# Five-block rounds for all groups, and attention scores from rounded parts after the eighth job

## Chip, cores, metric

The kernel runs on one core of a Trainium2 chip. The metric is the device time of one execution in microseconds (us), the median of several executions. All tensors in memory are float32. On TensorE a product can be taken in full float32, which runs as two passes, or on operands in F32R, a rounded form of float32, in one pass.

## What is computed

An attention whose softmax keeps only scores within `tau` of the row's maximum, and then two dense two-layer networks on its output. Batch 4, 8 heads, 576 positions, head width 64; 2304 tokens, model width 512, inner width 2048.

```python
scores = scale * np.matmul(q, k.transpose(0, 1, 3, 2))
thresh = np.max(scores, axis=-1, keepdims=True) - tau
scores = np.where(scores >= thresh, scores, -1000000000.0)
attn = np.exp(scores - np.max(scores, axis=-1, keepdims=True))
attn = attn / (np.sum(attn, axis=-1, keepdims=True) + 1e-09)
x = np.matmul(attn, v)                    # -> (2304, 512)
h = x @ w_in                              # first network
x = np.where(h >= 1, h, np.where(h <= -1, 0.0, (h + 1) ** 2 / 4)) @ w_out
h = x @ w_in2                             # second network
out = (h * np.clip(h + 3.0, 0.0, 6.0) / 6.0) @ w_out2
```

## The kernel before

**Attention** is cut into 16 jobs, numbered from 0: one batch and one pair of heads each. A job has five blocks of queries: four of 128 and a last one of 64. For a block, `em_scores` takes the products of queries and keys in float32 (line 335). The two heads lie on the two halves of the 128 partitions, so a product uses 64 rows of TensorE's array, and the two heads' products, which write to different PSUM banks, are issued in turn. In the fifth block each product uses a quarter of the array (64 rows, 64 columns). VectorE then takes the row minimum of the negated scores (348), ScalarE the exponential (360), VectorE masks and sums (369), TensorE turns the result (284), ScalarE copies it out (397), and TensorE multiplies by the values (433).

Queries and keys have to be turned before a job. Jobs 0 to 3 (`JT = 4`) do this on TensorE with 5 and 6 transposes, and ScalarE copies the result out of PSUM. From job 4 on they are loaded in strips 32 wide (`strips`, line 227, twelve DMA issues per job), VectorE's 32x32 transposes turn them (lines 293 and 309), and GpSimd scales the queries (295).

**Dense layers.** Every dense product is made of three products of rounded parts: high x high, high x low, low x high. Weights are loaded and split into parts `wih`, `wil`, `woh`, `wol` by `split_a` and `split_b` (ScalarE 118, 121 or 125 and 139; VectorE 129 and 135; GpSimd 122, 137 and 141). Raw weights stand in a ring of `RAW` = 3 buffers, and of `MORE` = 2 others while attention runs. `split_x` splits the inputs (ScalarE 656, VectorE 657).

**Beside attention**, once job 3 is done, the first network's first ten inner blocks of 128 (`NF1 = 10`) are worked off for six groups of 256 tokens. `em_h` makes an inner block (twelve products of 256 columns, line 676, then the activation, 685 to 694, with high and low parts `gh`, `gl`). `em_part` adds it to one half of the model width (six products, line 738) in the one PSUM bank Q3. When a round's last inner block is in, the bank is emptied and stored as `x2p`; a round that continues an earlier one first loads the earlier sum into `before` and adds it (747). `ROUNDS` lists the rounds in order. The list `steps` says which halves follow which inner block, at a distance set by `OFF`; from it follows `HOLD`, the number of buffers of `gh` and of `gl`, which is 12.

**Afterwards** the rest of the first network and the second network run on 512 tokens at a time (lines 676 and 718).

**Order of work.** Each engine runs its instructions in order. `attention()` and `dense1()` are generators that are stepped alternately; a scheduler then orders the instructions of each engine by priority and by when its own model has them ready. Pins (`after`, `pin_mlp`) tie some of them together. All loads and stores here go through SyncE's queue in order.

Of the kernel before, what the change touches and what calls it, by code (L numbers as in the profile page):

```python
# [8 lines left out]
F32 = mybir.dt.float32  # L9
F32R = mybir.dt.float32r  # L10
ACTF = mybir.ActivationFunctionType
ALU = mybir.AluOpType
# [6 lines left out]
def kernel(  # L19
# [13 lines left out]
    V, S, G, T = nc.vector, nc.scalar, nc.gpsimd, nc.tensor  # L33
    NB, NH, SEQ, D = q.shape
# [4 lines left out]
    MAIN = 512  # L39
    TAIL = SEQ - MAIN  # L40
    HS = SEQ // 2
    GRP = 256

    NG = (NB - 1) * MAIN // GRP
# [2 lines left out]
    NW = len(WIDE)  # L47
    NF1 = 10
    NAT = 1
    JT = 4  # L50
    MLAG = 2
    RAW = 3
    MORE = 2

    const = ctx.enter_context(tc.tile_pool(name="const", bufs=1))
    wbase = ctx.enter_context(tc.tile_pool(name="wbase", bufs=1))
# [7 lines left out]
    taus = const.tile([128, 4], F32, name="taus")  # L64
# [9 lines left out]
    def f32(ap):  # L74
        return ap.bitcast(F32)
# [130 lines left out]
    ap = att_es.enter_context(tc.tile_pool(name="att", bufs=1))  # L206
    mode = {"mlp": False, "att": True, "step": False, "t": 0, "s": 0, "n": 0}

    qn = ap.tile([128, 5, 128], F32, name="qn")
    kn = ap.tile([128, 5, 128], F32, name="kn")  # L210
    vn = [ap.tile([128, 5, 2, D], F32, name=f"vn{i}") for i in range(2)]
    qt, kt = {}, {}
    rp = ap.tile([128, 32], F32, name="rp")
    rq = ap.tile([128, 32], F32, name="rq")
    G.memset(rp, 0.0)
# [18 lines left out]
    def load_q(j):  # L234
        if j >= NJ:
            return
        E = nc.sync if j else nc.scalar
        b, hp = jobs[j]
        for h in HEADS:
            src = q[b, 2 * hp + h]  # L240
            if j >= JT:
                strips(qn, 0, src, h)
                continue
            E.dma_start(out=qn[:, 0:4, h * D:(h + 1) * D], in_=rows(src, b))
        if j < JT:
            E.dma_start(out=qn[0:TAIL, 4, :].rearrange("p (h d) -> p h d", h=2), in_=both(q, j))
# [27 lines left out]
    readers = {}  # L274
# [5 lines left out]
    def reads(x, ago=0):  # L280
        readers[(mode["s"] - ago) % 2] = x

    def turn(out, in_, pin):
        x = T.transpose(out, in_, ident)  # L284
        if pin:
            pe_pins.append(x)

    def unit_q(j):
        if j >= NJ or j in qt:
            return  # L290
        qt[j] = ap.tile([128, SEQ], F32, tag="qt", name="qt", bufs=2)
        if j >= JT:
            V.transpose(out=qt[j], in_=qn.rearrange("p c n -> p (c n)")[:, 0:SEQ])
            load_q(j + 1)
            G.tensor_scalar(out=qt[j], in0=qt[j], scalar1=taus[:, 1:2], scalar2=None, op0=ALU.mult)
            return
        tm = unit_bank().rearrange("p e n -> p (e n)")
        for c in range(5):
            turn(tm[:, c * 128:(c + 1) * 128], qn[:, c, :], c == 0)
        load_q(j + 1)  # L300
        reads(S.activation(out=qt[j], in_=tm[:, 0:SEQ], func=ACTF.Copy, scale=taus[:, 1:2]))

    def unit_k(j):

        if j >= NJ or j in kt:
            return
        kt[j] = ap.tile([128, SEQ + TAIL], F32, tag="kt", name="kt", bufs=2)
        if j >= JT:
            V.transpose(out=kt[j], in_=kn.rearrange("p c n -> p (c n)"))
            load_k(j + 1)  # L310
            return
        tm = unit_bank().rearrange("p e n -> p (e n)")
        for i, c in enumerate((4, 0, 1, 2, 3, 4)):
            turn(tm[:, i * 128:(i + 1) * 128], kn[:, c, :], i == 0)
        load_k(j + 1)
        reads(S.activation(out=kt[j], in_=tm[:, 128 - TAIL:128 + MAIN + TAIL], func=ACTF.Copy))
# [4 lines left out]
    def em_scores(j, i):  # L321

        last = i == NBLK - 1

        if not last:
            mode["s"] += 1
        ss = [unit_bank() for _ in range(1 if last else 2)]
        prev = None
        c = slice(i * 128, i * 128 + (TAIL if last else 128))
        for x, (h, e) in enumerate(((0, 0), (1, 1), (0, 1), (1, 0)) if last else ((0, 0), (1, 0), (0, 1), (1, 1))):  # L330
            r = slice(h * D, (h + 1) * D)
            k0 = e * HS + (TAIL if last or h == 0 else 0)
            o = ss[0][h * TAIL:(h + 1) * TAIL, e, 0:HS] if last else ss[h][:, e, 0:HS]
            with tc.high_priority(offset=900 if x else 0):
                mm = T.matmul(o, qt[j][r, c], kt[j][r, k0:k0 + HS], start=True, stop=True, skip_group_check=True)  # L335
            after(mm, prev)
            prev = mm
            if x == 0:
                pe_pins.append(mm)
                for y in range(1 if last else 2):  # L340
                    after(mm, readers.get((mode["s"] - y) % 2), True)
        nm = ap.tile([128, 2], F32, tag="nm", name="nm", bufs=3)
        th = ap.tile([128, 2], F32, tag="th", name="th", bufs=3)
        p = ap.tile([128, 2, 2, HS], F32, tag="p", name="p", bufs=3)
        if i == 0:
            zt[j] = ap.tile([128, 9], F32, tag="z", name="z", bufs=2)
        for x, s in enumerate(ss):
            reads(V.tensor_scalar(out=p[:, x], in0=s[:, :, 0:HS], scalar1=-1.0, scalar2=3e38,  # L348
                                           op0=ALU.mult, op1=ALU.min, accum_out=nm[:, x:x + 1]), len(ss) - 1 - x)
        blk[j, i] = (p, nm, th, [])  # L350

# [437 lines left out]
                nc.sync.dma_start(out=out[b * SEQ + MAIN:(b + 1) * SEQ, :], in_=ob[64 * e:64 * e + 64, :])  # L789

    HALF = NF1 // 2
    ROUNDS = [(g, list(range(f, f + HALF))) for f in (0, HALF) for g in range(2)]
    ROUNDS += [(g, list(range(NF1))) for g in range(2, NG)]
    before = {}
    hs = [(r, f) for r, (g, fs) in enumerate(ROUNDS) for f in fs]
    n_h = len(hs)
    outs = [(r, half, f) for r, (g, fs) in enumerate(ROUNDS) for half in range(2) for f in fs]
    OFF = NF1 + 2 * MLAG - 3
    steps, o = [], 0
    while o < len(outs):  # L800
        n = len(steps)
# [94 lines left out]
    V.tensor_scalar(out=taus[:, 3:4], in0=taus[:, 2:3], scalar1=0.0, scalar2=3e38, op0=ALU.is_lt, op1=ALU.mult)  # L896
    V.tensor_scalar(out=taus[:, 1:2], in0=taus[:, 2:3], scalar1=0.0, scalar2=0.125, op0=ALU.is_ge, op1=ALU.mult)
    V.tensor_tensor(out=taus[:, 0:1], in0=taus[:, 2:3], in1=taus[:, 3:4], op=ALU.max)
    warm = [None]

    def warm_up(n):
# [38 lines left out]
    for _ in attention():  # L940
# [11 lines left out]
        while credit > 0:  # L952
            c = next(part1)
# [98 lines left out]
```

## Time and profile before

| | us |
|---|---|
| median of three runs | 1119.1 (1118.22 to 1119.16) |
| profiled execution, its own time | 1118.67 |
| its span, first to last instruction | 1116.9 |
| mean granted clock of TensorE | 0.992 |

| engine | busy us | share of the span |
|---|---|---|
| TensorE matmul (PE) | 1087.4 | 97% |
| TensorE weight load (PEld) | 882.1 | 79% |
| VectorE (DVE) | 583.3 | 52% |
| ScalarE (ACT) | 614.0 | 55% |
| GpSimd (POOL) | 438.4 | 39% |

Busy time is that in which at least one instruction of the engine is recorded. Matmuls are pipelined, so their records overlap: how long one occupies the engine is the distance from its start to the next start, not its duration. Each record of a float32 product is one pass, so the 320 score products have 640 records. The shares are means over stages with different limits; the stretches of the profile tell more.

### The profile page before, as it was taken

The numbers are of one execution on the slowest core, as the hardware profiler recorded it, in microseconds if no ns is written. First come the engines' busy times: TensorE is split into PE (matmuls) and PEld (weight loads), VectorE is DVE, ScalarE is ACT, GpSimd is POOL, SyncE is SP. The second block draws the span as 40 slices with busy tenths as digits, with TensorE's granted clock in tenths as the row PEclk, the third lists the DMA queues.
The fourth block names the chain that finished last, engine by engine and source line by source line (L and its number), as shares of the span: only waits on it lengthen the run. The fifth ranks groups of instructions, "written<-read, shape, count | busy, mean of one in ns | idle before, by whom it ended". The sixth has DMA issues, their size and how long they took to land.

```text
span 1116.9 us, 17595 instructions
## 1 busy us (share of the span) xinstructions
PE 1087.4 (97%) x6478; PEld 882.1 (79%) x6478; DVE 583.3 (52%) x1204; ACT 614.0 (55%) x1215; POOL 438.4 (39%) x382
## 2 busy tenths in 40 slices
PE   7998889999999999999999999999999999999998
PEld 5555667777878877888889888888888888898886
DVE  5899887876666656355536765558411111211111
ACT  5777886866667666556557766555432222333222
POOL 0233767622222111155627566567522222222221
PEclk9999889999999999999999999999999999999999
DMA  6454445433222110025222544533010110010001
GB/s 165 118 100 107 124 120 150 103 93 74 63 59 62 43 43 22 12 67 170 77 94 78 157 143 145 158 114 111 24 38 1 33 38 1 10 38 8 13 1 38
DMA packets 140230, 84.26 MB, mean 75 GB/s; under 512 B 99440, under 2 KB 123248, under 8 KB 140144
## 3 DMA queue, kind: packets, MB, share of 16 engines
q1 hardware_dynamic: 138800, 82.84, 27.0%
q8 instruction: 51, 0.84, 0.3%
q10 hardware_dynamic: 1344, 0.30, 0.1%
q14 instruction: 35, 0.29, 0.1%
HBM read 65.73 MB, written 17.37 MB: 74 GB/s over the span
## 4 chain that ended last, share of the span: by engine, by line
PE 88%; DVE 7%; ACT 2%; POOL 1%; issue 1%; SPq 1%; DMA 0%; DVEq 0%; POOLq 0%; ACTq 0%
PE Q L676 35%; PE P L718 28%; PE Q L738 7%; PE Q L433 6%; PE P L335 6%; PE Q L284 5%; DVE p L348 2%; DVE p L369 2%; ACT e L360 1%; DVE xl L657 1%; SPq L227 0%; PE Q L904 0%; DVE th L363 0%; DVE w_c L135 0%; DMA w_raw<-in_moe_w_out_dram 0%
## 5 line engine op out<-in xcount | busy, mean ns | idle before, releaser
L694 POOL TENSOR_TENSOR gl<-r,gh 128x512 fp32r<-128x512 f32 (+1 forms) x190 | 202.6, 1067 | 501.0 <-ACT gh L693 500.5
L676 PE MATMUL Q<-xh,wih 128*128 128x512 f32 (+1 forms) x760 | 262.0, 345 | 0.9 <-DVE r L687 0.7
L676 PE MATMUL Q<-xl,wih 128*128 128x512 f32 (+1 forms) x760 | 257.1, 338 | 0.0
L676 PE MATMUL Q<-xh,wil 128*128 128x512 f32 (+1 forms) x760 | 256.8, 338 | 0.0
L690 DVE SCALAR_TENSOR_TENSOR r<-r,Q 128x512 f32<-128x512 f32 (+1 forms) x80 | 50.7, 633 | 249.4 <-ACT r L689 249.3
L693 ACT ACTIVATE gh<-r 128x512 fp32r<-128x512 f32 (+1 forms) x190 | 99.9, 526 | 125.3 <-PE P L718 53.2
L676 PEld LDWEIGHTS Q<-xh,wih 128*128 128x128 f32 x760 | 144.1, 190 | 24.3 <-issue 4.2
L676 PEld LDWEIGHTS Q<-xl,wih 128*128 128x128 f32 x760 | 144.2, 190 | 16.0
L676 PEld LDWEIGHTS Q<-xh,wil 128*128 128x128 f32 x760 | 144.0, 190 | 15.5
L348 DVE TENSOR_SCALAR_CACHE_REDUCE p<-P 128x576 f32<-128x576 f32 x144 | 104.0, 751 | 53.3 <-PE Q L284 41.0
L369 DVE SCALAR_TENSOR_TENSOR p<-p,th,e 128x576 f32<-128x576 f32 x144 | 122.8, 873 | 15.1 <-ACT e L360 9.5
L689 ACT ACTIVATE r<-Q,three 128x512 f32<-128x512 f32 (+1 forms) x80 | 51.4, 643 | 142.9 <-PE Q L676 138.3
L360 ACT ACTIVATE e<-p,nm 128x576 f32<-128x576 f32 x144 | 108.9, 775 | 34.5 <-DVE p L348 33.6
L687 DVE SCALAR_TENSOR_TENSOR r<-r,Q 128x256 f32<-128x256 f32 (+1 forms) x110 | 54.8, 498 | 125.7 <-ACT r L686 122.4
L284 PE MATMUL Q<-ident,p 128*128 128x128 f32 x656 | 107.9, 282 | 9.8 <-ACT Gf L397 6.5
L718 PE MATMUL P<-woh,gh 128*128 128x512 f32 x288 | 111.9, 390 | 0.6 <-DVE ob L776 0.6
L718 PE MATMUL P<-wol,gh 128*128 128x512 f32 x288 | 112.2, 390 | 0.0
L718 PE MATMUL P<-woh,gl 128*128 128x512 f32 x288 | 111.0, 390 | 0.0
L335 PE MATMUL P<-kt,qt 64*128 64x288 f32 (+1 forms) x640 | 99.5, 429 | 11.0 <-DVE p L348 9.0
L284 PEld LDWEIGHTS Q<-ident,p 128*128 128x128 f32 x656 | 73.6, 141 | 46.3 <-ACT Gf L397 14.0
L137 POOL TENSOR_TENSOR w_c<-w_c,w_raw 128x512 int32<-128x512 int32 x64 | 89.5, 1400 | 41.3 <-DVE w_c L135 23.0
L397 ACT ACTIVATE Gf<-Q 128x512 f32<-128x512 f32 x128 | 74.4, 596 | 33.5 <-PE Q L284 32.8
(91 smaller groups left out, 1840.1 us busy)
## 6 DMA issues: line engine op xcount, KB each, us to landing
w_raw<-in_moe_w_in_dram SPq DMA_DIRECT2D x32, 512.0 KB
w_raw<-in_moe_w_out_dram SPq DMA_DIRECT2D x32, 512.0 KB
vn<-in_v_dram SPq DMA_DIRECT2D x32, 128.0 KB
x2p<-ob SPq DMA_DIRECT2D x16, 256.0 KB
x2d<-ob SPq DMA_DIRECT2D x16, 256.0 KB
xst<-x2d SPq DMA_DIRECT2D x16, 256.0 KB
out_dram<-ob SPq DMA_DIRECT2D x16, 256.0 KB
xst<-xd SPq DMA_DIRECT2D x15, 256.0 KB
```

Of the source, the lines that this page charges most:

```text
L137: x = G.tensor_tensor(out=c.bitcast(I32), in0=c.bitcast(I32), in1=r, op=ALU.add)
L284: x = T.transpose(out, in_, ident)
L335: mm = T.matmul(o, qt[j][r, c], kt[j][r, k0:k0 + HS], start=True, stop=True, skip_group_check=True)
L348: reads(V.tensor_scalar(out=p[:, x], in0=s[:, :, 0:HS], scalar1=-1.0, scalar2=3e38, op0=ALU.mult, op1=ALU.min, accum_out=nm[:, x:x + 1]), ...
L360: pins["S"] = S.activation(out=e, in_=p[:, x], func=ACTF.Exp, bias=nm[:, x:x + 1], scale=-1.0)
L369: pins["M"] = V.scalar_tensor_tensor(out=p[:, x], in0=p[:, x], scalar=th[:, x:x + 1], in1=e, op0=ALU.is_le, op1=ALU.mult, accum_out=zt[j][ ...
L397: S.activation(out=f[:, h, :, d0:d0 + 128], in_=tm.rearrange("p (c n) -> p c n", c=4), func=ACTF.Copy)
L676: mm = T.matmul(h, l[:, kk * 128:(kk + 1) * 128], r, start=(x == 0), stop=(x == 3 * KD - 1))
L693: x = S.activation(out=gh, in_=r, func=ACTF.Copy)
L694: y = G.tensor_tensor(out=gl, in0=r, in1=f32(gh), op=ALU.subtract)
L718: T.matmul(a, l, r, start=(first and x == 0), stop=(last and x == 2))
L738: mm = T.matmul(o, l, r, start=(f == fs[0] and x == 0 and i == 0), stop=(f == fs[-1] and x == 2 and i == 1), skip_group_check=True)
```

## The change

`JT` goes from 4 to 8: jobs 4 to 7 turn queries and keys on TensorE too. From job 8 on, `split_t` turns an operand on VectorE into a buffer `raw`, ScalarE copies it rounded (`qt`, `kt`), and GpSimd subtracts to get the low part (`ql`, `kl`). GpSimd's scaling of the queries goes; the factor moves into the negation after the scores (`taus[:, 3:4]`). A block's scores are then three rounded products for each one before: `qt` x `kt`, `qt` x `kl`, `ql` x `kt`. In the fifth block the two heads' queries stand in one operand with zeros beside them, so that a product uses the whole array.

`ROUNDS` now gives each of the six groups two rounds of five inner blocks, two groups in turn. `OFF` is 9, and `HOLD` comes out as 8. `MORE` is 1: one raw weight buffer less while attention runs.

```diff
-    JT = 4
+    JT = 8
...
-    MORE = 2
+    MORE = 1
...
             if j >= JT:
-                strips(qn, 0, src, h)
+                strips(qn, 0, src[0:MAIN, :], h)
+                strips(qn, 16 + 2 * h, src[MAIN:SEQ, :], h)
...
+    def split_t(nat, hi, name):
+        raw = ap.tile([128, SEQ + TAIL], F32, tag="raw", name="raw")
+        lo = ap.tile([128, SEQ + TAIL], F32R, tag=name, name=name, bufs=2)
+        V.transpose(out=raw, in_=nat.rearrange("p c n -> p (c n)"))
+        S.activation(out=hi, in_=raw, func=ACTF.Copy)
+        G.tensor_tensor(out=lo, in0=raw, in1=f32(hi), op=ALU.subtract)
+        return lo
...
-            V.transpose(out=qt[j], in_=qn.rearrange("p c n -> p (c n)")[:, 0:SEQ])
+            ql[j] = split_t(qn, qt[j], "ql")
             load_q(j + 1)
-            G.tensor_scalar(out=qt[j], in0=qt[j], scalar1=taus[:, 1:2], scalar2=None, op0=ALU.mult)
...
-            V.transpose(out=kt[j], in_=kn.rearrange("p c n -> p (c n)"))
+            kl[j] = split_t(kn, kt[j], "kl")
...
+        thirds = j >= JT
+        whole = thirds and last
+        terms = ((qt, kt), (qt, kl), (ql, kt)) if thirds else ((qt, kt),)
+        for pair in (((0, 0),), ((0, 1),)) if whole else (es[0:2], es[2:4]):
+            for n, (a, w) in enumerate(terms):
+                for h, e in pair:
+                    r = slice(0, 128) if whole else slice(h * D, (h + 1) * D)
...
+                        mm = T.matmul(o, a[j][r, cs], w[j][r, k0:k0 + HS], start=(n == 0), stop=(n == len(terms) - 1),
+                                      skip_group_check=True)
...
-    ROUNDS = [(g, list(range(f, f + HALF))) for f in (0, HALF) for g in range(2)]
-    ROUNDS += [(g, list(range(NF1))) for g in range(2, NG)]
+    ROUNDS = [(g, list(range(f, f + HALF))) for b in range(NG // 2) for f in (0, HALF) for g in (2 * b, 2 * b + 1)]
...
-    OFF = NF1 + 2 * MLAG - 3
+    OFF = 9
```

The order in which TensorE gets its instructions shows at three places. First the scores of the first block of job 9; `P_3206` and `P_3207` are the PSUM tiles of the two heads. Before:

```order
L335 MATMUL P_3206<-kt,qt 128x288
L335 MATMUL P_3207<-kt,qt 128x288
L335 MATMUL P_3206<-kt,qt 128x288
L335 MATMUL P_3207<-kt,qt 128x288
L284 MATMUL Q_3067<-ident,p 128x128 x4
```

In the changed kernel the same block, with the heads' tiles `P_3297` and `P_3298`:

```order
L356 MATMUL P_3297<-kt,qt 128x288
L356 MATMUL P_3298<-kt,qt 128x288
L356 MATMUL P_3297<-kl,qt 128x288
L356 MATMUL P_3298<-kl,qt 128x288
L356 MATMUL P_3297<-kt,ql 128x288
L356 MATMUL P_3298<-kt,ql 128x288
L356 MATMUL P_3297<-kt,qt 128x288
L356 MATMUL P_3298<-kt,qt 128x288
L356 MATMUL P_3297<-kl,qt 128x288
L356 MATMUL P_3298<-kl,qt 128x288
L356 MATMUL P_3297<-kt,ql 128x288
L356 MATMUL P_3298<-kt,ql 128x288
```

Two products per head became six, still in turn between the heads. Second, the fifth block of job 8 on TensorE, between products of `em_part`. Before:

```order
L738 MATMUL Q_2931<-gh,wol_2580 128x256
L335 MATMUL P_3073<-kt,qt 64x288 x4
L284 MATMUL Q_2989<-ident,p 128x128 x4
L738 MATMUL Q_2931<-gh,woh_2579 128x256
L738 MATMUL Q_2931<-gl,woh_2579 128x256
```

In the changed kernel, with `P_3176` as the PSUM tile of both heads:

```order
L762 MATMUL Q_2949<-gh,wol_2717 128x256
L356 MATMUL P_3176<-kt,qt 128x288
L356 MATMUL P_3176<-kl,qt 128x288
L356 MATMUL P_3176<-kt,ql 128x288
L356 MATMUL P_3176<-kt,qt 128x288
L356 MATMUL P_3176<-kl,qt 128x288
L356 MATMUL P_3176<-kt,ql 128x288
L285 MATMUL Q_3105<-ident,p 128x128
```

Four products on quarters of the array became six on the whole of it. Third, TensorE ahead of the scores of job 6, where `kn` are the keys as loaded. Before, VectorE turns them, and TensorE has only the work of earlier blocks there:

```order
L738 MATMUL Q_1738<-gl,woh_1488 128x256
L738 MATMUL Q_1738<-gh,wol_1489 128x256
L284 MATMUL Q_1752<-ident,p 128x128 x4
L335 MATMUL P_1921<-kt,qt 128x288
L335 MATMUL P_1922<-kt,qt 128x288
```

In the changed kernel:

```order
L285 MATMUL Q_1746<-ident,p 128x128
L285 MATMUL P_1899<-ident,kn 128x128 x6
L457 MATMUL Q_1750<-Gf,vn_97 64x256 x8
L457 MATMUL Q_1750<-Gt,vn_97 64x256 x2
L285 MATMUL Q_1790<-ident,p 128x128 x4
L356 MATMUL P_1931<-kt,qt 128x288
```

The six transposes of the keys (`P_1899`) are added ahead of the scores; the five of the queries stand some twenty rows earlier.

## Rows read from the trace of the kernel before

**Rows 1.** Busy time by stretch: us, then busy us (instructions) of each engine
```profile
0.00:107.00 107.00, 94.38 (x661) 60.32 (x661) 87.51 (x238) 78.02 (x158) 27.73 (x35) 1.00 0.52 122
107.00:210.00 103.00, 91.26 (x638) 69.41 (x638) 88.22 (x195) 79.91 (x176) 72.97 (x62) 0.92 0.51 132
210.00:470.00 260.00, 258.96 (x2021) 208.06 (x2019) 162.29 (x438) 169.15 (x376) 61.63 (x64) 1.00 0.22 54
...
520.00:1117.00 597.00, 592.80 (x2881) 500.88 (x2879) 215.47 (x295) 257.48 (x450) 251.13 (x203) 1.00 0.21 65
```

**Rows 2.** Waits of TensorE, 107 to 210 us: total, times, longest
```profile
PE Q L284 <- ACT Gf L397: 4.0, 5, 1.6
PE P L335 <- DVE p L348: 3.4, 2, 2.1
...
PE Q L738 <- DVE ob L751: 1.4, 1, 1.4
```

**Rows 3.** Waits of TensorE, 210 to 470 us
```profile
PE Q L676 <- DVE r L687: 0.7, 2, 0.5
```

**Rows 4.** Timeline of TensorE around a fifth block: start us, us
```profile
233.73 0.28 PE L676 MATMUL Q<-xh,wil 128*128 128x256 f32 x1
...
234.09 0.28 PE L676 MATMUL Q<-xh,wil 128*128 128x256 f32 x1
...
234.56 0.37 PE L738 MATMUL Q<-gh,woh 128*128 128x256 f32 x1
...
234.88 0.28 PE L738 MATMUL Q<-gh,wol 128*128 128x256 f32 x1
235.09 1.19 PE L335 MATMUL P<-kt,qt 64*64 64x288 f32 x8
...
236.62 0.36 PE L738 MATMUL Q<-gh,woh 128*128 128x256 f32 x1
```

**Rows 5.** Timeline of TensorE, first and last of nine products of 512 columns
```profile
639.65 0.39 PE L676 MATMUL Q<-xh,wil 128*128 128x512 f32 x1
...
641.46 0.39 PE L676 MATMUL Q<-xl,wih 128*128 128x512 f32 x1
```

**Rows 6.** Timeline of TensorE and its weight loads in another block
```profile
302.98 1.24 PE L335 MATMUL P<-kt,qt 64*128 64x288 f32 x8
...
303.33 0.65 PE L335 MATMUL P<-kt,qt 64*128 64x288 f32 x4
...
303.57 0.65 PE L335 MATMUL P<-kt,qt 64*128 64x288 f32 x4
...
303.33 0.44 PEld L335 LDWEIGHTS P<-kt,qt 64*128 64x128 f32 x4
```

**Rows 7.** Timeline of TensorE before job 3, transposes
```profile
64.32 0.82 PE L284 MATMUL P<-ident,kn 128*128 128x128 f32 x6
64.98 0.71 PE L284 MATMUL Q<-ident,p 128*128 128x128 f32 x5
```

**Rows 8.** Groups by form: count, busy us, mean ns, idle before
```profile
L694 POOL TENSOR_TENSOR gl<-r,gh 128x512 fp32r<-128x512 f32 x98 | 131.0, 1338 | 267.5 <-ACT gh L693 267.2
...
L657 DVE TENSOR_TENSOR xl<-xu,xh 128x256 fp32r<-128x256 f32 x29 | 12.8, 474 | 1.7 <-ACT xh L656 1.7
...
L309 DVE STREAM_TRANSPOSE kt<-kn 128x640 f32<-128x640 f32 x12 | 9.7, 805 | 0.1
...
L316 ACT ACTIVATE kt<-P 128x640 f32<-128x640 f32 x4 | 2.9, 724 | 0.7 <-PE P L284 0.7
```

**Rows 9.** Chain of work that ended last, 60 to 215 us: start us, us
```profile
103.22 0.69 DVE qt L293
103.92 0.72 DVE kt L309
...
133.10 3.86 DMA w_raw<-in_moe_w_out_dram
...
165.05 2.20 POOL qt L295
```

More of the change, by code (lines that the diff above doesn't have):

```diff
@@ L211 @@
     vn = [ap.tile([128, 5, 2, D], F32, name=f"vn{i}") for i in range(2)]
-    qt, kt = {}, {}
+    qt, kt, ql, kl = {}, {}, {}, {}
     rp = ap.tile([128, 32], F32, name="rp")
@@ L290, in unit_q @@
             return
-        qt[j] = ap.tile([128, SEQ], F32, tag="qt", name="qt", bufs=2)
+        qt[j] = ap.tile([128, SEQ + TAIL], F32R if j >= JT else F32, tag="qt", name="qt", bufs=2)
         if j >= JT:
-            V.transpose(out=qt[j], in_=qn.rearrange("p c n -> p (c n)")[:, 0:SEQ])
+            ql[j] = split_t(qn, qt[j], "ql")
             load_q(j + 1)
-            G.tensor_scalar(out=qt[j], in0=qt[j], scalar1=taus[:, 1:2], scalar2=None, op0=ALU.mult)
             return
@@ L300, in unit_q @@
         load_q(j + 1)
-        reads(S.activation(out=qt[j], in_=tm[:, 0:SEQ], func=ACTF.Copy, scale=taus[:, 1:2]))
+        if j == JT - 1:
+            G.memset(qn[0:64, 4, 64:128], 0.0)
+            G.memset(qn[64:128, 4, 0:64], 0.0)
+        reads(S.activation(out=qt[j][:, 0:SEQ], in_=tm[:, 0:SEQ], func=ACTF.Copy, scale=taus[:, 1:2]))
     def unit_k(j):
@@ L306, in unit_k @@
             return
-        kt[j] = ap.tile([128, SEQ + TAIL], F32, tag="kt", name="kt", bufs=2)
+        kt[j] = ap.tile([128, SEQ + TAIL], F32R if j >= JT else F32, tag="kt", name="kt", bufs=2)
         if j >= JT:
-            V.transpose(out=kt[j], in_=kn.rearrange("p c n -> p (c n)"))
+            kl[j] = split_t(kn, kt[j], "kl")
             load_k(j + 1)
@@ L329, in em_scores @@
         c = slice(i * 128, i * 128 + (TAIL if last else 128))
[L330 to L341, printed above, removed]
+        thirds = j >= JT
+        whole = thirds and last
+        es = ((0, 0), (1, 1), (0, 1), (1, 0)) if last else ((0, 0), (1, 0), (0, 1), (1, 1))
+        terms = ((qt, kt), (qt, kl), (ql, kt)) if thirds else ((qt, kt),)
+        x = 0
+        for pair in (((0, 0),), ((0, 1),)) if whole else (es[0:2], es[2:4]):
+            for n, (a, w) in enumerate(terms):
+                for h, e in pair:
+                    r = slice(0, 128) if whole else slice(h * D, (h + 1) * D)
+                    k0 = e * HS + (TAIL if last or h == 0 else 0)
+                    if whole:
+                        o, cs = ss[0][:, e, 0:HS], slice(MAIN, MAIN + 128)
+                    else:
+                        o, cs = ss[0][h * TAIL:(h + 1) * TAIL, e, 0:HS] if last else ss[h][:, e, 0:HS], c
+                    with tc.high_priority(offset=900 if x else 0):
+                        mm = T.matmul(o, a[j][r, cs], w[j][r, k0:k0 + HS], start=(n == 0), stop=(n == len(terms) - 1),
+                                      skip_group_check=True)
+                    after(mm, prev)
+                    prev = mm
+                    if x == 0:
+                        pe_pins.append(mm)
+                        for y in range(1 if last else 2):
+                            after(mm, readers.get((mode["s"] - y) % 2), True)
+                    x += 1
         nm = ap.tile([128, 2], F32, tag="nm", name="nm", bufs=3)
@@ L347, in em_scores @@
         for x, s in enumerate(ss):
-            reads(V.tensor_scalar(out=p[:, x], in0=s[:, :, 0:HS], scalar1=-1.0, scalar2=3e38,
+            reads(V.tensor_scalar(out=p[:, x], in0=s[:, :, 0:HS],
+                                           scalar1=taus[:, 3:4] if j >= JT else -1.0, scalar2=3e38,
                                            op0=ALU.mult, op1=ALU.min, accum_out=nm[:, x:x + 1]), len(ss) - 1 - x)
@@ L898 @@
     V.tensor_tensor(out=taus[:, 0:1], in0=taus[:, 2:3], in1=taus[:, 3:4], op=ALU.max)
+    V.tensor_scalar(out=taus[:, 3:4], in0=taus[:, 1:2], scalar1=-1.0, scalar2=None, op0=ALU.mult)
     warm = [None]
```

## The prediction

> **What bounds the kernel now.** I read the stages first, from the view of busy time by stretch. Attention has the chip to itself until about 107 us, it gets company from the first dense layer until about 470, and from there on everything is dense. In [rows 1] the reader is to see TensorE: 94.4 of 107 us, then 91.3 of 103 with a mean granted clock of 0.92, then 259.0 of 260 and 592.8 of 597. In the second stretch VectorE is busy for 88.2 of 103 us and GpSimd for 73.0, far more than later. I call 107 to 210 us the ramp: weights are split there while the first dense groups already wait for them.
>
> Second, who makes TensorE wait. In the ramp these are single stalls of up to 2 us behind ScalarE and VectorE [rows 2]. From 210 to 470 us there are two entries, the larger of 0.7 us [rows 3]. So from 210 us on each matmul removed or added moves the end by what it occupies, and other engines count only if they become late enough to stop TensorE. Before 210 us an engine's time counts where it lies on the chain of work.
>
> Third, what a matmul occupies. Busy time does not tell this, because records overlap; distances between starts do. A rounded (F32R) matmul of 256 columns takes (234.09 - 233.73)/3 = 0.12 us [rows 4], one of 512 columns (641.46 - 639.65)/8 = 0.226 us [rows 5]. Scores in full float32 run as two passes, in pairs: the two heads on the two halves of the array's rows start together, and the next pair of passes starts 0.24 us later (303.33 to 303.57) [rows 6].
>
> **Scores of jobs 8 to 15.** These 40 blocks lie from 210 to 450 us, where TensorE is full. What a block costs today: from the product at 234.88 to that at 236.62 lie 1.74 us; the same stretch without scores (one rounded product and four transposes, 234.09 to 234.56) takes 0.47; so a block takes 1.27 us [rows 4]. Four pair slots of 0.24 make 0.96 of it. The other 0.31 us is the price of a visit: entering and leaving the mode with the array cut in two.
>
> A changed block has six pair slots of one pass. Nothing in the trace shows a rounded matmul on half of the rows. From the two rounded prices, 288 columns take 0.120 + 32/256 x (0.226 - 0.120) = 0.133 us. The bounds are 0.12 (half of a float32 pass pair) and 0.266 (the two heads one after the other). I take 0.133, because the float32 pairs run side by side without loss: 6 x 0.133 = 0.80 us in place of 0.96. Four cut blocks in each of eight jobs: 32 x 0.16 = **5.1 us less**. The fifth block of a job becomes six whole-array products, also 0.80 us, with no visit: 8 x (1.27 - 0.80) = **3.8 us less**. The order lists hold 104 runs in the cut mode before and 94 after; eight of the ten are those blocks, two more merge: 2 x 0.31 = **0.6 us less**.
>
> One thing could spoil the short slots: each pass needs its own weights. In [rows 6] the loads for the next passes start at 303.33 with the running passes on the same rows and are over by 303.77, before the passes that need them at 303.81 or so: they are hidden. Only the first load after the mode change shows, 0.35 - 0.24 = 0.11 us. With slots of 0.133 a load of 0.11 still fits, but barely.
>
> The Trainium skill (TensorE: Matmul & The Clock Gate, "The mechanism") states that a weight load overlaps running matmuls only when it goes to another row group. The float32 passes here don't bear that out, since their loads overlap on the same rows; no row shows it for rounded halves. By the rule each slot would hold 0.133 + 0.11 us, and the sum would come out slower; I count that as a rival below.
>
> **Transposes of jobs 4 to 7.** JT = 8 moves four jobs' queries and keys from VectorE's transposes to TensorE: 5 + 6 per job, 44 in all. Six take 64.98 - 64.32 = 0.66 us [rows 7], so 44 x 0.11 = **4.8 us more**, part before 107 us and part in the ramp. ScalarE's two copies replace VectorE's two transposes (about 0.72 against 0.80 us each [rows 8]). VectorE is on the chain with them at 103 us: 0.69 + 0.72 = 1.4 us [rows 9]. Those I count as **1.4 us less**. The bounds of this gain are nothing and all eight transposes, 8 x 0.80 = 6.4 us; I stay low, since at the other three jobs I don't find the pair next to each other on the chain.
>
> **Preparing the parts (jobs 8 to 15).** Per operand one transpose of 0.80 us on VectorE, one copy of about 0.72 on ScalarE, and one subtraction on GpSimd, by the subtraction of 128x512 about 1.338 x 640/512 = 1.67 us [rows 8]. GpSimd loses the scaling of the queries (2.2 us in the ramp [rows 9]). One buffer "raw" serves both operands, so they go one after the other: 2 x (0.80 + 0.72 + 1.67) = 6.4 us. The order lists prepare a job's operands while the job before it is scored, some 25 us ahead, so that is covered; uncovered it would be 6.4 us per job. ScalarE gains 16 x 0.72 = 11.5 us, against 91 us free from 210 to 470 [rows 1]. Cost: nothing.
>
> **Rounds.** Groups 2 to 5 now take two rounds each. No matmul is added. Added are 16 splits of inputs (VectorE 0.47 us each [rows 8], 7.6 us, ScalarE about as much), eight more emptied accumulators with their stores, and eight loads of earlier sums. VectorE has 98 us free there, so these are hidden if they come in time. The load has some 7 us (five half steps of six products, 0.72 us each, and 2.5 inner blocks of twelve, 1.44 us each) before its sum is needed; a weight load twice its size takes 3.9 us [rows 9]. The price where it fails: 1.4 us, the one visible wait for an emptied bank [rows 2]. Taken: nothing; bounds nothing and 8 x 1.4 = 11 us.
>
> **One weight buffer less.** Today five weights are loaded ahead. A late load costs up to 3.9 us [rows 9], an early one nothing. Four ahead still cover about 25 us at the ramp's pace (16 weights in 103 us), so I take nothing. The plain loads of jobs 4 to 7 also spare SyncE's queue the strips, which I price at nothing, since TensorE's waits don't name it.
>
> **The sum.** 5.1 + 3.8 + 0.6 + 1.4 - 4.8 = 6.1 us less. The profiled execution took 1118.67 us for a span of 1116.9, and the median of the runs is 1119.1; less 6.1 this gives 1112.6 against the one and 1113.0 against the other. I forecast **1113 us**.
>
> **Rivals.**
> *Short slots don't stay short* (slower). If loads are exposed, 32 x 6 = 192 slots grow by 0.11 us: +21.1, so 1134 us. If the heads run one after the other, by 0.133: +25.5, so 1138.5 us. It turns the change into a loss from a slot of 0.133 + 6.1/192 = 0.165 us on. For it: a slot leaves 0.02 us of slack. Against it: the float32 pairs. Chance 0.13.
> *The ramp grows.* GpSimd gets 2 x 1.67 us for job 8 in place of 2.2, a weight comes late once (3.9), and the clock, whose 0.92 cost (1 - 0.92) x 103 = 8.2 us, drops for a third as long again (2.7): +7.7, so 1121 us. For it: VectorE at 86% and GpSimd at 71% there. Against it: jobs 5 to 7 relieve both. Chance 0.15.
> *The ramp shrinks*: all of VectorE's eight transposes turn into time, 6.4 - 1.4 = 5.0 us more gained, so 1108 us. For it: the waits on VectorE in [rows 2]. Chance 0.12.
> *Banks empty late*: three waits of 1.4 us for sums that aren't loaded, so 1117 us. Chance 0.10.
>
> **How the numbers follow.** The forecast has 0.50, and a range of its own of 1109 to 1116. The shrinking ramp reaches to about 1105, the growing one and the late banks to 1122; beyond lie the long slots (0.13) and tails of 0.06. So the range is 1105 to 1122. Within 0.2% of 1119.1 is 1116.9 to 1121.3, about what a measurement of this kernel can tell from no change. Faster: 0.50 + 0.12 + 0.04 of the growing ramp + 0.04 of the late banks = 0.70. Same: 0.06 + 0.06 = 0.12. Slower: 0.13 + 0.05 = 0.18.
>
> **What will show it.** Cut blocks of jobs 8 to 15 with pair starts 0.13 us apart, and the fifth block 0.80 us from its first product to the next work. Job 8's scores starting within 4 us of 210. TensorE's waits from 210 to 470 still about 1 us, with no new entry for an emptied bank. I am wrong if pair starts lie 0.17 us or more apart, or if job 8 starts after 216 us.

## The result, and the profile after

| | before | after |
|---|---|---|
| median, us | 1119.13 | 1125.26 |
| lowest to highest of four runs | 1118.22 to 1119.73 | 1124.6 to 1126.52 |
| span of the profiled execution | 1116.9 | 1123.8 |

By the medians the changed kernel is slower by 6.1 us; the ratio is 1.0061, its 95% interval 1.0048 to 1.0073. The forecast was 6.1 us faster.

The stretches first, in the columns of [rows 1]:

```profile
0.00:107.00 107.00, 94.72 (x679) 61.42 (x680) 84.47 (x232) 80.21 (x162) 22.87 (x33) 1.00 0.45 114
107.00:210.00 103.00, 84.30 (x602) 63.73 (x601) 83.56 (x178) 76.39 (x161) 62.52 (x56) 0.97 0.48 127
210.00:470.00 260.00, 253.77 (x2148) 217.70 (x2147) 190.32 (x479) 190.83 (x426) 78.90 (x77) 0.99 0.28 72
```

In the ramp TensorE is busy for 84.3 us in place of 91.3. Part of this is its higher mean clock (0.97 against 0.92): in these traces it worked at the lower level for 14.1 us before and 6.8 us after, and half of the difference, some 3.6 us, is time that the same work no longer takes. Every other engine is busy for less time too, so none became the bound there; more of the stretch is spent waiting. From 210 to 470 us TensorE has 6.2 us free, where it had 1.0 before. Who it waits for, from 107 to 210 us and then from 210 to 245:

```profile
PE P L285 <- DVE p L371: 3.5, 2, 2.2
PE Q L285 <- ACT Gf L421: 3.5, 3, 2.1
PE Q L700 <- DVE r L711: 2.9, 3, 1.4
PE P L356 <- DVE p L371: 2.2, 3, 1.0
PE Q L762 <- DVE ob L775: 2.1, 2, 1.5
PE Q L457 <- ACT Gf L424: 2.1, 1, 2.1
...
PE Q L285 <- ACT xu L463: 2.5, 1, 2.5
PE P L356 <- DVE p L371: 1.9, 1, 1.9
```

The first row is new against [rows 2]: the transposes of queries and keys (285) wait for a PSUM bank that VectorE's row minimum (371) has not yet emptied. From 245 to 470 us only 0.7 us of waits are left. From 160 to 240 us, where the table below puts most of the added loss, the largest rows name other work:

```profile
PE Q L285 <- ACT xu L463: 3.7, 2, 2.5
PE Q L700 <- DVE r L711: 2.8, 3, 1.4
PE Q L762 <- DVE ob L775: 2.1, 2, 1.5
...
PE P L285 <- DVE p L371: 1.3, 1, 1.3
```

So TensorE waits there for several kinds of ScalarE's and VectorE's work, and the transposes' bank is 1.3 us of it.

What a matmul occupies came out as forecast. First a block of job 9, then a fifth block, in the timeline of TensorE:

```profile
256.86 0.28 PE L762 MATMUL Q<-gh,wol 128*128 128x256 f32 x1
257.06 0.40 PE L356 MATMUL P<-kt,qt 64*128 64x288 f32 x2
257.30 0.30 PE L356 MATMUL P<-kl,qt 64*128 64x288 f32 x2
257.44 0.30 PE L356 MATMUL P<-kt,ql 64*128 64x288 f32 x2
257.57 0.30 PE L356 MATMUL P<-kt,qt 64*128 64x288 f32 x2
257.71 0.29 PE L356 MATMUL P<-kl,qt 64*128 64x288 f32 x2
257.84 0.29 PE L356 MATMUL P<-kt,ql 64*128 64x288 f32 x2
258.06 0.66 PE L285 MATMUL Q<-ident,p 128*128 128x128 f32 x4
...
279.79 0.29 PE L356 MATMUL P<-kt,qt 128*128 128x288 f32 x1
...
280.58 0.27 PE L285 MATMUL Q<-ident,p 128*128 128x128 f32 x1
```

Pairs start (257.84 - 257.30)/4 = 0.135 us apart, and the fifth block takes 280.58 - 279.79 = 0.79 us. Only the first slot after the mode change is longer, 0.24 us.

To set work against waiting I priced every start of a TensorE instruction by what it occupies at the full clock: 0.12, 0.133 and 0.227 us for rounded products of 256, 288 and 512 columns, 0.24 for a float32 pair, 0.11 for a transpose, 0.155 for each entry to or exit from the array cut in two. What lies between starts beyond that is lost time. Work and lost time are estimates by these prices, good to some 0.5 us.

| us | work | lost | lost 0-110 | 110-160 | 160-240 | after 240 |
|---|---|---|---|---|---|---|
| before | 1065.6 | 45.6 | 21.0 | 13.6 | 7.8 | 3.1 |
| after | 1060.4 | 57.5 | 17.8 | 14.9 | 18.9 | 6.0 |

The change took 5.2 us of work off TensorE, as forecast (its terms of work add up to 5.1 + 3.8 + 0.6 - 4.8 = 4.7), and added 11.9 us in which TensorE has nothing ready or runs at the lower clock. Of this 11.1 us lie from 160 to 240 us, 1.3 from 110 to 160 and 2.9 behind 240, against 3.2 saved before 110 us.

### The profile page after: what moved, and what is told of

Read it like the earlier page. It is cut to its first block, busy times and chain, and to the rows that moved or that the text cites. A ratio compares the mean times of both kernels' runs of the same rounds, so it can differ in the third digit from the quotient of the medians.

```text
span 1123.8 us, 18063 instructions
## 1 busy us (share of the span) xinstructions
PE 1082.1 (96%) x6634; PEld 892.0 (79%) x6634; DVE 604.5 (54%) x1221; ACT 635.1 (57%) x1255; POOL 440.5 (39%) x388
## 4 chain that ended last, share of the span: by engine, by line
PE 78%; DVE 8%; ACT 6%; issue 3%; POOL 3%; DMA 2%; SPq 0%; DVEq 0%; POOLq 0%; ACTq 0%
PE Q L700 30%; PE P L742 25%; PE Q L457 6%; PE P L356 6%; PE Q L762 6%; PE Q L285 5%; DVE p L371 2%; DVE p L393 2%; POOL w_c L137 1%; ACT e L384 1%; DVE w_c L135 1%; ACT Gf L421 1%; POOL gl L718 1%; DMA qn<-in_q_dram 1%; ACT r L709 1%
## 5 line engine op out<-in xcount | busy, mean ns | idle before, releaser
L393 DVE SCALAR_TENSOR_TENSOR p<-p,th,e 128x576 f32<-128x576 f32 x144 | 127.9, 912 | 15.8 <-ACT e L384 9.4
L356 PE MATMUL P<-kt,qt 64*128 64x288 f32 (+2 forms) x464 | 78.1, 407 | 11.0 <-DVE p L371 9.0
L762 PE MATMUL Q<-gh,woh 128*128 128x256 f32 x240 | 75.1, 313 | 2.4 <-DVE ob L775 2.1
```

Source lines behind the costliest of these rows:

```text
L356: mm = T.matmul(o, a[j][r, cs], w[j][r, k0:k0 + HS], start=(n == 0), stop=(n == len(terms) - 1), skip_group_check=True)
L393: pins["M"] = V.scalar_tensor_tensor(out=p[:, x], in0=p[:, x], scalar=th[:, x:x + 1], in1=e, op0=ALU.is_le, op1=ALU.mult, accum_out=zt[j][ ...
L762: mm = T.matmul(o, l, r, start=(f == fs[0] and x == 0 and i == 0), stop=(f == fs[-1] and x == 2 and i == 1), skip_group_check=True)
```

## Experiments

Theory at the start: the transposes and the shorter ring of `gh` and `gl` make TensorE wait in the ramp, while the scores gain as forecast. Rivals: the new order of rounds itself, the weight buffer, and the preparation of parts. A ratio is to the kernel before on the same chip, with its 95% interval; that kernel had medians of 1118.4 to 1118.8 us beside these runs.

**The parts of the change by themselves.** First the changed kernel with jobs 4 to 7 turned by VectorE again (`JV = 4`):

```diff
-        if j < JT:
+        if j < JV:
...
+        if j >= JV:
+            x = qt[j][:, 0:SEQ]
+            V.transpose(out=x, in_=qn.rearrange("p c n -> p (c n)")[:, 0:SEQ])
+            load_q(j + 1)
...
+            G.tensor_scalar(out=x, in0=x, scalar1=taus[:, 1:2], scalar2=None, op0=ALU.mult)
+            return
```

> The changed kernel, but jobs 4 to 7 load strips and turn queries and keys on VectorE, with GpSimd's scaling, as before; jobs 8 to 15, rounds and buffers as changed. The changed kernel took 1125.3 us. Theory 1 (the turning on TensorE lengthens the ramp: its transposes wait 3.5 us for a bank that VectorE frees, beside 4.8 us of work): 1113 to 1117. Theory 2 (the rounds with the ring of eight), theory 3 (one weight buffer less) and theory 4 (the parts prepared in the ramp): the 4.8 us of transposes at most come back, 1120 to 1125.

1119.22 us, 1.0007 [0.9999, 1.0016]. I call this the first variant. So in the changed kernel the turning on TensorE costs about 6 us (1.0061 against 1.0007). That is the price of all that goes with `JT`: the transposes, ScalarE's copies, and plain loads in place of strips; no run takes these apart.

The kernel before with the new rounds alone:

```diff
-    ROUNDS = [(g, list(range(f, f + HALF))) for f in (0, HALF) for g in range(2)]
-    ROUNDS += [(g, list(range(NF1))) for g in range(2, NG)]
+    ROUNDS = [(g, list(range(f, f + HALF))) for b in range(NG // 2) for f in (0, HALF) for g in (2 * b, 2 * b + 1)]
-    OFF = NF1 + 2 * MLAG - 3
+    OFF = 9
```

> The kernel before with the new rounds, OFF = 9 and the ring of eight alone; float32 scores, turning on VectorE from job 4, MORE = 2. Theory 2 (the rounds lengthen the ramp): 1125 to 1132. Theories 1, 3 and 4: 1117 to 1121, as before.

1125.86 us, 1.0068 [1.0055, 1.0080]. That is 7.3 us slower, where I had forecast nothing. Against it the first variant (1119.22 us), which adds the scores from rounded parts, gains 6.6 us.

One raw weight buffer less alone (`MORE = 1`):

```diff
-    MORE = 2
+    MORE = 1
```

> The kernel before with MORE = 1 alone, one raw weight buffer less during attention. Theory 3 (weights come late): 1123 to 1130. Theories 1, 2 and 4: 1117 to 1121, as before.

1117.82 us, 0.9998 [0.9989, 1.0007]: nothing, as forecast.

The transposes alone (`JT = 8`, float32 scores kept):

```diff
-    JT = 4
+    JT = 8
```

> The kernel before with JT = 8 alone: jobs 4 to 7 are turned on TensorE, jobs 8 to 15 as before on VectorE with float32 scores. Theory 1 (beside 4.8 us of transposes the ramp grows by the wait for banks and what follows): 1127 to 1133. Theories 2 to 4: 4.8 us of work less some relief of VectorE, 1121 to 1124.

1127.68 us, 1.0083 [1.0069, 1.0096]: 9.1 us slower, where the two terms that belong to it said 4.8 - 1.4 = 3.4. In the profiled execution the span grew by 7.8 us: work by about 5 (44 transposes at 0.11 are 4.8), lost time by about 3. Its largest wait is that of the transposes for VectorE's row minimum, here as a wait row from 107 to 135 us:

```profile
PE P L284 <- DVE p L348: 4.3, 1, 4.3
```

**What in the rounds costs 7.3 us.** Three runs of the kernel before with the new `ROUNDS`, with either distance and either ring. Distance 9 with the old ring of twelve:

```diff
+    OFF = 9
...
+    HOLD = 12
```

> The kernel before with the new rounds and OFF = 9 alone, but with rings of 12 in place of 8 for gh and gl. The same with rings of 8 took 1125.9 us, the kernel before 1118.6. Ring theory (TensorE runs out of inner blocks it may make while second-layer weights are late): 1118 to 1121. Order theory (OFF = 9 asks for second-layer weights a step earlier, and moves the splits): 1124 to 1127. Third theory (the added splits and sums of groups 2 to 5): 1124 to 1127.

1125.17 us, 1.0053 [1.0040, 1.0065]. Distance 11 (as before), and the ring of nine that follows from it:

```diff
+    OFF = 11
```

> The kernel before with the new rounds, OFF = 11 as before, and the ring of 9 that follows from it. Ring theory: 1123 to 1126. Order theory: 1118 to 1121. Third theory: 1124 to 1127.

1123.18 us, 1.0036 [1.0024, 1.0049]. Distance 11 and a ring of twelve:

```diff
+    OFF = 11
...
+    HOLD = 12
```

> The kernel before with the new list of rounds alone: OFF = 11 and rings of 12, as before. Up to 210 us its work is that of the kernel before. Ring theory and order theory: 1118 to 1121. Third theory (added splits and sums): 1124 to 1127.

1121.65 us, 1.0026 [1.0016, 1.0035]. The ring is the smaller part: with distance 9, twelve buffers in place of eight bring 0.7 us, with distance 11, twelve in place of nine bring 1.5. With the ring of twelve the list alone costs 3.0 us, and distance 9 another 3.5, with 9.0 us lost from 160 to 210 us in place of 5.9. Some of the list's price at distance 11 shows long after attention, in the timeline of TensorE in the last of these runs, where the kernel before has no wait:

```profile
552.61 0.50 PE L718 MATMUL P<-gl,woh 128*128 128x512 f32 x1 [0.28 <-POOL gl L694]
...
564.62 0.50 PE L718 MATMUL P<-gl,woh 128*128 128x512 f32 x1 [0.21 <-POOL gl L694]
```

Lost time behind 540 us is 1.7 us more than before there, and from 400 to 470 us about 1 us more. With distance 9 it is within 0.5 us of before behind 540 us, so these waits are no part of the 7.3 us; of the list's other cost I found no single place.

**Do the prices carry over to the scores from rounded parts?** The first variant with distance 11 and `MORE = 0` for room:

```diff
-    MORE = 1
+    MORE = 0
...
-    OFF = 9
+    OFF = 11
```

> The changed kernel with jobs 4 to 7 turned on VectorE as before, OFF = 11, the ring of 9 that follows, and MORE = 0 (two raw weight buffers less than before, to make room). With OFF = 9, a ring of 8 and MORE = 1 it took 1119.2 us. Order theory: 1110 to 1114. Ring theory: 1117 to 1120. If the parts prepared in the ramp cost what the rounds don't: 1113 to 1117.

1128.02 us, 1.0082 [1.0068, 1.0095]. The run says little on distance, since a weight comes late. Its chain of work (start, length, what):

```profile
172.18 3.86 DMA w_raw<-in_moe_w_out_dram
...
176.06 0.67 ACT w_raw L119
176.73 0.36 ACT r L723
...
177.53 0.49 ACT Gf L435
```

ScalarE stands at the weight for 3.6 us, and `Gf`, for which TensorE waits, is queued behind it. Four buffers cost nothing in the run with `MORE = 1` alone; here, with three, a weight is late. No run has three buffers and nothing else changed.

Distance 10, with a ring of eight and four weight buffers:

```diff
-    OFF = 9
+    OFF = 10
```

> The first variant without transposes on TensorE in jobs 4 to 7 (1119.2 us), with OFF = 10 in place of 9; HOLD stays 8. Theory that OFF = 9 brings output weights forward among the splits and so delays TensorE from 160 to 210 us: half of the 2.7 to 3.5 us between OFF 9 and 11 comes back, about 1117.6 us, and TensorE's lost time from 160 to 240 us falls by 1 to 3 us. Theory that the distance costs nothing in itself with scores from rounded parts, since the parts' preparation is what is late there: 1119 us again.

1121.49 us, 1.0026 [1.0016, 1.0036], 2.3 us slower where 1.6 faster was expected. Its work on TensorE is that of distance 9 (1055.9 us). Its clock stood at the lower level for 27 us before 260 us, that of distance 9 for 20 us; at half speed the difference is 3.4 us. What let the clock fall longer there is not shown.

Distance 11, with one buffer of `ql` for room:

```diff
-        lo = ap.tile([128, SEQ + TAIL], F32R, tag=name, name=name, bufs=2)
+        lo = ap.tile([128, SEQ + TAIL], F32R, tag=name, name=name, bufs=2 if name == "kl" else 1)
...
-    OFF = 9
+    OFF = 11
```

> The same variant with OFF = 11 and a HOLD of 9; the room comes from one buffer of ql in place of two, and MORE stays 1. Order theory: the gain seen between the rounds alone at OFF 9 and 11, 2.7 us, so 1116.5 us; that would be under both kernels. If the single buffer of ql makes GpSimd wait for the last product of the job before, the scores of a job's first block wait for ql: up to 1 us for each of eight jobs, so up to 1124 us.

1121.11 us, 1.0024 [1.0015, 1.0033]. No wait for `ql` shows, but TensorE's order now breaks the scores into 85 unbroken runs in place of 79, and its work is 2.8 us more. (The 85 and 79 count a fifth block on the whole array as a run too; it is the six added runs that are visits to the cut array.) So neither distance 10 nor 11 came out faster with these scores. But this run does not settle whether distance 9 has a price of its own: from 160 to 240 us it loses about 11 us where the first variant loses 14, which is what the order theory expected, and more visits, and some 2 us more lost behind 540 us, take that back.

**Half of the transposes.** The kernel before with `JT = 6`:

```diff
-    JT = 4
+    JT = 6
```

> The kernel before with JT = 6 alone: jobs 4 and 5 turn queries and keys on TensorE, float32 scores stay. With JT = 8 this cost 9.1 us. Theory that each added transpose has one price (9.1 us over 44): half, 4.6 us, so 1123.2 us. Theory that the transposes are cheap while attention is alone, where TensorE has gaps and VectorE is on the chain, and dear in the ramp, where they wait in TensorE's order for a bank that VectorE empties: 0 to 1.5 us, so 1118.6 to 1120 us.

1125.02 us, 1.0059 [1.0047, 1.0072]. Both theories miss: 6.4 us is neither half of 9.1 nor next to nothing. Work rises by 3.0 us and lost time falls by 3.0 from 60 to 110 us, but it rises by 4.6 from 110 to 160 us and by 1 to 1.5 from 160 to 240 us. From 107 to 135 us this trace has a wait as long as the one in the run with `JT = 8`, here of the scores:

```profile
PE P L335 <- DVE p L348: 5.7, 3, 4.3
```

Only these two traces have a wait of 4.3 us for the row minimum there. In the others, that of the kernel before included, the longest is 2.0 to 2.2 us, and the changed kernel's 2.2 us is no longer; what is new there is that transposes stand and wait, and that the waits of transposes and scores for the row minimum add up to 5.7 us in the ramp (3.5 and 2.2) in place of 3.4 [rows 2]. How such a wait comes about can be followed. Timeline of VectorE, GpSimd and TensorE after:

```profile
121.64 1.22 DVE L135 SCALAR_TENSOR_TENSOR w_c<-w_raw,w_c 128x512 uint32<-128x512 uint32 x1
...
122.93 1.28 POOL L137 TENSOR_TENSOR w_c<-w_c,w_raw 128x512 int32<-128x512 int32 x1 [0.63 <-DVE w_c L135]
123.10 1.74 DVE L393 SCALAR_TENSOR_TENSOR p<-p,th,e 128x576 f32<-128x576 f32 x1
...
124.17 1.79 POOL L141 TENSOR_TENSOR wol<-w_c,woh 128x512 fp32r<-128x512 f32 x1
...
124.76 1.81 DVE L393 SCALAR_TENSOR_TENSOR p<-p,th,e 128x576 f32<-128x576 f32 x1
124.81 0.28 PE L762 MATMUL Q<-gl,woh 128*128 128x256 f32 x1
125.92 1.78 POOL L141 TENSOR_TENSOR wil<-w_c,wih 128x512 fp32r<-128x512 f32 x1
126.51 0.75 DVE L371 TENSOR_SCALAR_CACHE_REDUCE p<-P 128x576 f32<-128x576 f32 x1
127.32 0.77 PE L285 MATMUL P<-ident,qn 128*128 128x128 f32 x5 [2.23 <-DVE p L371]
...
128.52 0.82 DVE L393 SCALAR_TENSOR_TENSOR p<-p,th,e 128x576 f32<-128x576 f32 x1
```

Two maskings take 1.74 and 1.81 us in place of the 0.82 of the last row, each beside a step of GpSimd's weight split. Behind them stands the row minimum that empties the bank, and behind that on TensorE, in order, the transposes. The runs with `JT = 6` and `JT = 8` have the same pair of long maskings ahead of their 4.3 us. Long maskings as such are not new: from 107 to 210 us nine take more than 1 us in the kernel before and nine in the changed one. Then the clock falls, in stretches in the columns of [rows 1]:

```profile
125.00:128.40 3.40, 1.17 (x10) 0.97 (x9) 3.40 (x8) 1.23 (x3) 2.70 (x2) 1.00 0.55 154
128.40:131.80 3.40, 3.40 (x15) 2.00 (x14) 2.66 (x9) 3.40 (x8) 1.31 (x2) 0.50 0.38 87
```

TensorE idles for two thirds of 3.4 us and then works at 0.50, the level of 1.2 GHz, for 3.4 us: another 1.7 us. That the order on VectorE and GpSimd is the cause is read from traces and not shown; no run removed it by itself.

**Parts prepared in the ramp.** The first variant with scores from rounded parts from job 10 on in place of job 8:

```diff
-    JT = 8
+    JT = 10
```

> The first variant (1119.2 us) with scores from rounded parts from job 10 on in place of job 8. Theory that preparing the parts of jobs 8 and 9 costs about 2.8 us in the ramp: three quarters of the matmul gain stay (9.5 x 6/8 = 7.1 us of the rounds' 1125.9) and the loss goes, so 1118.7 us or less, with TensorE's lost time from 160 to 240 us back to about 12.8 us from 14.2. Theory that preparing costs the same in each of the eight jobs (total 6.7 us gained): 6.7 x 6/8 = 5.0 us, so 1120.9 us.

1117.72 us, 0.9994 [0.9985, 1.0003], as the theory of a loss in the ramp said. Work is 2.3 us more than with job 8, lost time 4.0 us less, most of it from 160 to 240 us. The parts themselves are not late: in the changed kernel VectorE turns job 8's queries from 170.62 us on, GpSimd ends the low part of its keys at 178.93 + 1.58 = 180.51 us, and its scores begin at 214.82 us. So what the parts cost there is not that scores wait for them; that it is the engines' time in the ramp, and what this pushes back, is argued.

The opposite, the changed kernel with all of it from job 4 on:

```diff
-    JT = 8
+    JT = 4
```

> The changed kernel with JT = 4: no transposes on TensorE in jobs 4 to 7, and scores from rounded parts from job 4 on, rounds as changed. Against the first variant (1119.2 us, parts from job 8 on) TensorE saves another 4 x 1.19 = 4.8 us. Theory that matmul work decides: 1114.4 us. Theory that the ramp is bound by the order on VectorE and GpSimd and that each job's parts cost about 1.4 us there: 1119.2 - 4.8 + 5.6 = 1120 us, with lost time from 60 to 210 us up by 5 us or more.

1127.85 us, 1.0076 [1.0062, 1.0090], slower than either theory said. Its TensorE has the least work of all, 1051.7 us, and it is the slowest of these but one: lost time is 68.5 us, 23 us more than before, of which some 10 or 11 lie between 60 and 160 us and as much between 160 and 240. VectorE is busy for 95 of the ramp's 103 us. So the ramp is bound by what the other engines hand to TensorE, not by TensorE's work.

**The scores alone, with the rounds of before.** Room for the ring of twelve comes from one buffer each for `ql` and `kl`, and from `raw` in a buffer of `p`:

```diff
-        raw = ap.tile([128, SEQ + TAIL], F32, tag="raw", name="raw")
-        lo = ap.tile([128, SEQ + TAIL], F32R, tag=name, name=name, bufs=2)
+        raw = ap.tile([128, 2, 2, HS], F32, tag="p", name="p", bufs=3).rearrange("p a b n -> p (a b n)")[:, 0:SEQ + TAIL]
+        lo = ap.tile([128, SEQ + TAIL], F32R, tag=name, name=name, bufs=1)
...
-    ROUNDS = [(g, list(range(f, f + HALF))) for b in range(NG // 2) for f in (0, HALF) for g in (2 * b, 2 * b + 1)]
+    ROUNDS = [(g, list(range(f, f + HALF))) for f in (0, HALF) for g in range(2)]
+    ROUNDS += [(g, list(range(NF1))) for g in range(2, NG)]
...
-    OFF = 9
+    OFF = 11
```

> The kernel before with scores from rounded parts from job 10 on and nothing else that counts: rounds, OFF = 11 and HOLD = 12 as before, jobs 4 to 9 turned by VectorE as before, MORE = 1 (shown to cost nothing). For room ql and kl have one buffer each and raw stands in a buffer of p. Theory that the scores' gain is real and the rounds' loss goes with the rounds: 9.5 x 6/8 = 7.1 us less than before, 1111.5 us, with pair starts of 0.133 us and TensorE's lost time near the 45.6 us of before. Theory that prices don't add, since any edit moves the order of VectorE and GpSimd in the ramp: the matmul work falls by 7.1 us, but lost time from 107 to 240 us rises by 3 us or more, so 1114.5 us or above. If the single buffers make scores wait for their parts: a new wait of scores for GpSimd, up to 3.3 us for each of six jobs, so up to 1131 us.

1116.55 us, 0.9979 [0.9970, 0.9988], under both kernels. But the work fell by 5.1 us and not by 7.1, and the trace shows where. Timeline of TensorE at the head of job 10:

```profile
281.30 0.40 PE L370 MATMUL P<-kt,qt 64*128 64x288 f32 x2
281.62 0.39 PE L714 MATMUL Q<-xh,wih 128*128 128x256 f32 x1
...
283.47 0.40 PE L370 MATMUL P<-kl,qt 64*128 64x288 f32 x2
```

The first pair runs, the cut array is left for twelve products of the dense layer and two transposes, and then entered again: the order places the pair ahead of `kl`, which has one buffer now.

The same from job 8 on:

```diff
-    JT = 10
+    JT = 8
```

> The same with scores from rounded parts from job 8 on. If preparing the parts of jobs 8 and 9 in the ramp costs what it saves (2.8 us against 2.4 us), it comes out within 1 us of its sister from job 10 on. If not, it is 2.4 us faster.

1120.57 us, 1.0023 [1.0013, 1.0034], 4 us slower than from job 10 on, more than expected, and 2.2 us slower than the kernel before: it loses 4.1 us more from 160 to 240 us than its sister. The order has 87 runs of scores in place of 85, but eight of them are fifth blocks on the whole array in place of six, so it enters the cut array no more often.

Last, the variant from job 10 on with the product of `kl` first, which brings the runs of scores back from 85 to 79, that is six visits to the cut array less:

```diff
-        terms = ((qt, kt), (qt, kl), (ql, kt)) if thirds else ((qt, kt),)
+        terms = ((qt, kl), (qt, kt), (ql, kt)) if thirds else ((qt, kt),)
```

> The variant with scores from rounded parts from job 10 on and the rounds of before (1116.55 us), with the three products of a score in another order: the one with kl first. In that variant TensorE's order enters and leaves the cut array 85 times instead of 79, since a job's first block begins before its kl is ready; with kl first it is 79 again. Theory that each visit has its price of 0.31 us: 6 x 0.31 = 1.9 us less, 1114.7 us. If TensorE then waits for kl at the head of the block, that comes back as waits of scores for GpSimd, up to 1.7 us in each of six jobs, and the time stays or grows, up to 1126 us.

1114.18 us, 0.9955 [0.9941, 0.9968]: 2.4 us less for six visits (1.9 expected), and 4.6 us under the kernel before. The 2.4 us are rough, since the executions of the sister spread from 1113.92 to 1118.13 us. It is the best of all. Its stretches:

```profile
107.00:210.00 103.00, 89.66 (x631) 68.64 (x630) 89.89 (x197) 79.43 (x174) 72.35 (x62) 0.92 0.52 131
210.00:470.00 260.00, 257.92 (x2145) 218.03 (x2142) 170.98 (x444) 179.78 (x397) 71.12 (x71) 1.00 0.24 57
```

The ramp is nearly that of [rows 1], and TensorE has 2.1 us free from 210 to 470 us, where it had 1.0 before.

## Why the prediction was wrong

What a product occupies on TensorE was forecast rightly. **Scores**: slots of 0.133 to 0.135 us against a forecast of 0.133; **fifth blocks**: 0.79 us against 0.80. The rival of slots that don't stay short falls. The Trainium skill (TensorE: Matmul & The Clock Gate, "The mechanism"), in its list of what overlaps, lets a weight load overlap only for another row group; here the loads of the next pair are hidden on the same rows, so the measurement decides against that sentence for this case. **A visit's price**, forecast at 0.31 us: the block above takes 258.06 - 256.86 - 0.12 = 1.08 us, 0.28 more than its six slots, and the last run gave 2.4/6 = 0.4 for each visit less, a rough figure. **One weight buffer less** was nothing, as forecast.

Three steps failed, all of them on what reaches TensorE in time in the ramp and just behind it:

- **Rounds, "Taken: nothing".** The list and its distance cost 7.3 us on their own. My argument was that VectorE has 98 us free from 210 to 470 us. But of the 6.9 us that the run with the rounds alone loses more than before, 3.3 lie from 160 to 210 us, and of the 3.0 from 210 to 470 most lie before 240. That I looked only at the whole stretch in which most of the new work is done is the error. With distance 9 output weights come forward among the splits (with rings of twelve, GpSimd's last step of a split at 122.0 us is for an output weight, where distance 11 has an input weight at 122.6), and VectorE is busy for 92.1 of the ramp's 103 us in the run with the rounds alone; that this order is what delays TensorE is argued, not shown. With rounded scores neither distance 10 nor 11 was faster, so 7.3 us is the price in this combination.
- **Transposes, "+4.8 less 1.4".** The work was right (4.5 us of it in the changed kernel) and the relief larger than taken (2.9 us less lost from 60 to 110 us). What I left out is that a transpose stands in TensorE's order and needs a PSUM bank that VectorE empties, 3.5 us of waits in the ramp. From 160 to 240 us 4.7 us came back as lost time, most of it waits for other work of ScalarE and VectorE. Measured: 6 us in the changed kernel, 9.1 us alone, against 3.4.
- **Preparing the parts, "Cost: nothing".** I had argued that the parts are ready some 25 us ahead. They are (job 8's by 180.5 us for scores at 214.8), and yet the cost is not nothing in the ramp: the scores brought 6.6 us with the changed rounds where the terms said 9.5, and moving the start to job 10 took 4.0 us off the lost time for 2.3 us more work. Behind the ramp it is nothing with two buffers (six jobs brought 1125.86 - 1117.72 = 8.1 us where the terms said 7.1); with the rounds of before and one buffer each, the best run brought 4.6 of these 7.1, and by the same prices it lost some 2.5 us more than before from 260 to 470 us.

From the kernel before at 1118.6 us over the rounds alone (1125.9) and the first variant (1119.2) to the changed kernel (1125.3), the steps are 7.3, -6.6 and 6; the forecast for them was 0, -9.5 and 3.4. That they add up is no proof, since each run stands on the one before it, and in another order the shares differ (the transposes alone cost 9.1). Among the rivals "the ramp grows" (1121 us) named the place; its price was too low, and two of its terms did not come true: the ramp's mean clock rose from 0.92 to 0.97, and no wait of TensorE for a weight stands among the rows above. One sign that I had set (job 8 after 216 us) was a poor one: job 8 starts at 214.8 us, but its second block only at 233.9, and job 9 at 257.1 us, 14.8 later than before (242.3). The other one spoke: TensorE's waits from 210 to 470 us were to stay about 1 us, and came to some 6. How much of the loss from 160 to 240 us belongs to which of the three edits stays open: by the same prices the rounds alone lose about 5 us more than before there and the turning on TensorE alone about 3, where the changed kernel loses 11 more, but every edit shifts the order on VectorE and GpSimd.

## What to carry to other kernels

Price a matmul by the distance between starts: here the forecasts held to about a hundredth of a microsecond (0.135 against 0.133, 0.79 against 0.80). But count it only where TensorE is full. In a stretch where four engines hand work to each other at 60 to 90% each, ask of every added instruction what stands behind it in its engine's order and which bank or buffer it must find empty. Try the parts of a bundle singly: here one of them, begun two jobs later and kept to one visit per block, is worth 4.6 us by itself, and with the changed rounds the scores from job 10 on are worth 0.9 (1117.72 us).

## What the hardware showed that I had not expected

In these traces VectorE and GpSimd stop each other. The kernel before has it too; first two rows that meet, then a step of GpSimd's split with only a short VectorE row beside it:

```profile
117.81 1.80 POOL L137 TENSOR_TENSOR w_c<-w_c,w_raw 128x512 int32<-128x512 int32 x1 [0.70 <-DVE w_c L135]
118.39 1.83 DVE L369 SCALAR_TENSOR_TENSOR p<-p,th,e 128x576 f32<-128x576 f32 x1
...
122.41 1.26 POOL L141 TENSOR_TENSOR wil<-w_c,wih 128x512 fp32r<-128x512 f32 x1
```

In the changed kernel the two maskings of 1.74 and 1.81 us above end at 124.84 and 126.57 us, 0.63 and 0.61 us after the ends of the GpSimd steps at 124.21 and 125.96 (start plus length), somewhat less than the 0.82 us that a masking takes by itself: as if each had begun in earnest only then. (In the kernel before it is 120.22 - 119.61 = 0.61 us.) GpSimd's next step, 1.78 us in place of 1.26, begins at 125.92 and gets its turn when the masking is over. The Trainium skill (SBUF — State Buffer, "SBUF: two separate sides") says that a VectorE instruction with two inputs in SBUF and a GpSimd instruction that reads SBUF exclude each other, and that the later one waits for the whole of the other. The trace agrees, but for the 0.2 us by which the masking's end comes sooner than a whole masking after GpSimd's.

Rounded products on 64 rows run as pairs at the price of one: 0.135 us for two of 288 columns, loads included, as long as the array stays cut; one on the whole array takes 0.79/6 = 0.13 us.
